# Nine of 24 units: y turned through DRAM and VectorE in place of TensorE

## The chip, the cores and the metric

The kernel runs on one core of one Trainium2 chip. The metric is device time in microseconds, from the start of the program to its end; the median of several runs is compared. A profiled execution also leaves a trace, whose span goes from its first to its last instruction.

## The reference

Two blocks are computed one after the other. The first is an mLSTM cell over `q`, `k`, `v` of shape (4, 8, 768, 40), with input, forget and output gates. At each time step and for each head:

```
m_new  = max(f + m, i)
C      = exp(f + m - m_new) * C + exp(i - m_new) * outer(v, k)
n      = exp(f + m - m_new) * n + exp(i - m_new) * k
y      = sigmoid(o) * (C q) / max(|n . q|, 1)
```

The y of all heads, 8 x 40 = 320 values for each of 4 x 768 = 3072 tokens, is the input x of a multiplicative feed-forward block with 1024 inner features, whose result (3072 x 320) is the output:

```
a, b = x @ w1, x @ w2
out  = ((a * b) @ w3) @ w_out
```

All is float32.

## The kernel before

**Tiling.** The cell works on units of 128 tokens of one batch: 6 chunks of 128 tokens by 4 batches make 24 units, numbered 0 to 23, batch fastest. Within a unit the recurrence is computed in two halves of 64 tokens: score matmuls within a half, a carried state between halves. Four units, one for each batch, make a group, so there are 6 groups. `w3 @ w_out` is folded once into `w3o`, so that the feed-forward block has an up stage (`up`, `up_rest`: a and b for pairs of feature tiles over 256 tokens, and their product `ab`) and a down stage (`ffn_out`: `po`, accumulated over the eight feature tiles for 128 tokens at a time).

**Steps.** One loop over s from 0 to 29 staggers all of this. In step s the cell begins unit s (scores and state, `quarter_work`) and ends unit s-1 (`outputs`, which writes y, 128 tokens by 320 values, at L382). Step s then holds, for earlier units, the turn of y, and feed-forward work set by the lists `n_up` and `n_down`: two up pieces a step from s = 7 to 28, and two down pieces a step from s = 17 to 26. Group 3 (units 12 to 15) is read by the up stage in steps 17 to 20, group 4 in steps 21 to 24, group 5 in steps 25 to 28; the first two steps of each read the group's first two units, the last two its other two. Step 29 holds the last four down pieces.

**The turn of y.** The up matmuls need x with features on partitions. In step s, `twice` (GpSimd, L386) writes the last 64 columns of unit s-2's y a second time, so that the 320 features make three tiles of 128. One step later `x_trans` turns the three tiles with TensorE (L93) into one PSUM tile `px`, and ScalarE copies it to `xT` (L396), which holds 512 tokens of a group and has two buffers.

**Other turns.** The q and k of the first 17 units are turned by TensorE (`turn`, `pt`). From unit 17 on (`N_DVE`), `load_turned` loads them with eight DMAs a unit into `turned_in` (single, in the tile `gates`), in an arrangement in which VectorE's transposes of 32x32 blocks finish the job (L287).

**PSUM.** The cell tile takes four banks. `mps` gives the other four, pool `ps_m`, to `px`, `pt`, `pa`, `pb`, `po` in turn. After step 24 the cell tile is closed and its four banks become a second pool, `ps_x`; from then `mps` takes the two pools by turns:

```
pool = banks.pop(0)
banks.append(pool)
return pool.tile(shape, FP, name=name, tag="m")
```

**What sets the order.** TensorE's order is the order of the program (`in_order`). The other engines' instructions, the DMA issues on SyncE's queue among them, are ordered by a scheduler from program order and its own estimate of when each is ready; each queue then runs in that order and waits at its head. In the first seven steps the program order is kept (`keep_order`). From step 1 to 24 the part after `quarter_work` that turns k and q on VectorE is held behind the last VectorE instruction of `outputs` (`issue_after(gated.ins)`). In the program, a step begins with the loads: weights for three units on (`load_u`, tile `pw`), k, q, v and the output gate two units on (`load`, `load_o`); `load_o` takes the buffer that y of unit s-2 frees. The y tile has two buffers, `o_sb`, which takes the result out, has two as well.

Of the kernel before, what the change touches and what calls it, by code (L numbers as in the profile page):

```python
# [8 lines left out]
FP = mybir.dt.float32  # L9
# [7 lines left out]
def kernel(  # L17
# [26 lines left out]
    nc = tc.nc  # L44
# [3 lines left out]
    P = 128  # L48
    NT = S // L
    NT2 = S // P  # L50
    NU = NT2 * B
# [3 lines left out]
    DM = H * D  # L55
# [3 lines left out]
    KF = DM // P  # L59
    REM = DM - KF * P  # L60
    GT = B
    TG = GT * P
# [5 lines left out]
    sb = ctx.enter_context(tc.tile_pool(name="sb", bufs=2))  # L68
    dram = ctx.enter_context(tc.tile_pool(name="dram", bufs=1, space=bass.MemoryType.DRAM))
# [39 lines left out]
    wT = const.tile([P, NT2, BH], FP, name="wT")  # L109
    decay = const.tile([P, B * NP, NT], FP, name="decay")  # L110
    U_d = dram.tile([NT, BH, L], FP, name="U_d")
    KC = KF + 1

    o_t, u_t = {}, {}

# [4 lines left out]
    def load(n):  # L120
        for dst, src in ((kbuf[n % NB][:, :, 0:D], k), (qbuf[n % NBQ][:, :, 0:D], q), (vbuf[n % NB][:, :, 0:D], v)):
            if src is not q or n < N_DVE:
                nc.sync.dma_start(out=dst, in_=rows(src, n))

    def load_turned(n):
        c, b = divmod(n, B)
        for dst, src in zip(turned_in, (k, q)):
            for hip in range(2):
                of = src[b].rearrange("(p two) s d -> two p s d", two=2)[hip, :, c * P:(c + 1) * P, :]
                for j in range(2):  # L130
                    p0, c0 = hip * DP + j * 32, (1 - j) * 32
                    nc.sync.dma_start(out=dst[p0:p0 + 32, c0:c0 + NP * RAW].rearrange("r (p e) -> r p e", p=NP),
                                      in_=of.rearrange("p (r f) d -> r p (f d)", f=4))

    def load_o(n):
        o_t[n] = io.tile([P, H, D], FP, name="o_in", tag="o_in", bufs=4)
        nc.sync.dma_start(out=o_t[n], in_=rows(o_gate, n))

    def load_u(n):
        c, b = divmod(n, B)  # L140
        src = U_d[2 * c:2 * c + 2, b * H:(b + 1) * H, :].rearrange("x h t -> x (h t)")
        for x in range(2):
            nc.sync.dma_start(out=weights_tile(n)[halves[x]].rearrange("p h t -> p (h t)"),
                              in_=src[x:x + 1].to_broadcast([L, H * L]))
# [77 lines left out]
    def scale_next():  # L222
        scaled.append(pend.pop(0))
        scale(scaled[-1][1])
# [17 lines left out]
    def fold():  # L242
        while ready_w3:
            w3_mm(ready_w3.pop(0))
        ready_w3.extend(turned_w3)
        turned_w3.clear()
# [9 lines left out]
    qT_t, kT_t, vw_t, before_t, y_t, x_t = {}, {}, {}, {}, {}, {}  # L256

    def out_gate(n):
        nc.scalar.activation(out=o_t[n], in_=o_t[n], func=AF.Tanh, scale=0.5)
# [11 lines left out]
    def weights(n):  # L271
        c, b = divmod(n, B)
        src = weights_tile(n) if c else spread(n)
        pw = weights_tile(n)
        for h in range(H):
            nc.scalar.activation(out=pw[:, h, :], in_=src[:, h, :], func=AF.Exp, bias=aT[:, c, b * H + h:b * H + h + 1])  # L276
        for r in halves:
            nc.gpsimd.affine_select(out=pw[r], in_=pw[r], compare_op=OP.is_ge, fill=0.0, base=0,  # L278
                                    pattern=[[0, H], [1, L]], channel_multiplier=-1)

    def turn(n):


        if n >= N_DVE:
            for src, dst, name in zip(turned_in, (kT_t, qT_t), ("kT", "qT")):
                dst[n] = sb.tile([128, NP, P], FP, name=name, tag=name)
                nc.vector.transpose(out=dst[n].rearrange("i p (r f) -> i p f r", f=4),  # L287
                                    in_=src[:, 32:TB].rearrange("i (p f d) -> i p f d", p=NP, f=4)[:, :, :, 0:32])
            return
        for src, dst, name in ((kbuf[n % NB], kT_t, "kT"), (qbuf[n % NBQ], qT_t, "qT")):  # L290
            pt = mps([128, NP, P], "pt")
            for p in range(NP):
                transpose(pt[:, p, :], src[:, 2 * p:2 * p + 2, :].rearrange("p a b -> p (a b)"))
            dst[n] = sb.tile([128, NP, P], FP, name=name, tag=name)
            nc.scalar.copy(out=dst[n], in_=pt)

    def weighted(n):
        c, b = divmod(n, B)
        vw_t[n] = sb.tile([P, H, D1], FP, name="vw", tag="vw")
        nc.gpsimd.tensor_tensor(out=vw_t[n], in0=vbuf[n % NB], op=OP.mult,  # L300
                                in1=wT[:, c, b * H:(b + 1) * H].unsqueeze(2).to_broadcast([P, H, D1]))

    def decayed(new, old, n, x):
        c, b = divmod(n, B)
        nc.gpsimd.tensor_tensor(out=new, in0=old, op=OP.mult, in1=decay[:, b * NP:(b + 1) * NP, 2 * c + x:2 * c + x + 1]  # L305
                                .to_broadcast([P, NP, D1]))
# [55 lines left out]
    def outputs(n, pi, ph):  # L362
# [6 lines left out]
        for x, r in enumerate(halves):  # L369
# [12 lines left out]
        return nc.vector.tensor_tensor(out=y_t[n][:, 0:DM].rearrange("p (h d) -> p h d", d=D), in0=h[:, :, 0:D], in1=e,  # L382
                                op=OP.mult)

    def twice(n):
        nc.gpsimd.tensor_copy(out=y_t[n][:, DM:DM + REM], in_=y_t[n][:, KF * P:DM])  # L386

    def x_trans(n):
        gr, j = divmod(n, GT)
        if j == 0:  # L390
            x_t[gr] = ffn.tile([128, KF + 1, TG], FP, name="xT", tag="xT")
        y = y_t.pop(n)
        px = mps([128, KF + 1, P], "px")
        for cc in range(KF + 1):
            transpose(px[:, cc, :], y[:, cc * P:(cc + 1) * P])
        nc.scalar.copy(out=x_t[gr][:, :, j * P:(j + 1) * P], in_=px)  # L396
# [119 lines left out]
    ffn = ctx.enter_context(tc.tile_pool(name="ffn", bufs=2))  # L516
# [27 lines left out]
    def ffn_out(gr, j):  # L544
        po = mps([P, DM], "po")
        for f in range(FO):
            mm(po, ab_t[gr][j // 2][:, f, j % 2 * P:(j % 2 + 1) * P], w3o[:, f, :], start=(f == 0), stop=(f == FO - 1))
        o_sb = ffn.tile([P, DM], FP, name="o_sb", tag="o_sb", bufs=2)
        nc.scalar.copy(out=o_sb, in_=po)  # L549
        t0 = j * S + gr * P  # L550
        nc.scalar.dma_start(out=out[t0:t0 + P, :], in_=o_sb)
# [13 lines left out]
    turned, converted, fetched = 0, 2, 2 * KF + 1  # L565

    for s in range(len(n_up)):
        if B <= s + 3 < NU:
            load_u(s + 3)
        if s + 2 < NU:  # L570
            load(s + 2)
            load_o(s + 2)
        if 0 < s < B - 1:
            weights(s + 1)
            out_gate(s)
        if s < NU:
            weighted(s)
            if s >= B:
                decayed(state[s % B][1], state[s % B][0], s, 0)
            if 0 < s < N_DVE:  # L580
                turn(s)
        if 0 <= s - 2 < NU:
            twice(s - 2)
        if N_DVE <= s + 1 < NU:
            load_turned(s + 1)
        while turned < min(s - 2, NU):
            x_trans(turned)
            turned += 1
        fold()
        for _ in range(n_down[s]):  # L590
            ffn_out(*downs.pop(0))
        now = [ups.pop(0) for _ in range(n_up[s])]
        open_ups = [up(*x) for x in now]
        if len(now) == 1 and turned == s - 2 < NU:
            x_trans(turned)
            turned += 1

        def rest():
            for x in open_ups:
                up_rest(*x)  # L600

        gated = None
        if s <= NU:
            gated = quarter_work(s, rest)
        else:
            rest()
        with tc.issue_after(gated.ins) if gated else nullcontext():
            if N_DVE <= s + 1 < NU:
                turn(s + 1)
        if s == 0:  # L610
            gate_cols(g, gT, nc.scalar.copy)
            out_gate(0)
            scale_next()
            weights(1)
        if s == NU:
            cell_psum.close()
            banks.append(ctx.enter_context(tc.tile_pool(name="ps_x", bufs=4, space=bass.MemoryType.PSUM)))
        if B - 1 <= s < NU:
            if s + 1 < NU:
                weights(s + 1)  # L620
            out_gate(s)
        for _ in range(n_cvt[s] if s < len(n_cvt) else 0):
            convert()
            converted += 1
        while todo and fetched < converted + (2 if s < 2 else 3):
            fetch(*todo.pop(0))
            fetched += 1
        if s + 1 == pinned:
            for ins in keep_order(front):
                behind.enter_context(tc.issue_after(ins))  # L630
# [30 lines left out]
```

## Time and profile before

| | us |
|---|---|
| median of 5 runs | 490.55 |
| lowest, highest run | 490.43, 492.9 |
| the profiled execution's own time | 492.14 |
| its span, first to last instruction | 490.4 |
| TensorE matmuls busy | 457.2 |
| VectorE busy | 261.0 |
| ScalarE busy | 146.3 |
| GpSimd busy | 88.2 |

The shares are averages over stages. Until about 230 us the weights are also loaded and converted on VectorE, and q and k are turned on TensorE; after that the steps are alike. In rows of groups of instructions, PE is a matmul and PEld the load of its stationary operand, DVE is VectorE, ACT ScalarE, POOL GpSimd and SPq SyncE's DMA queue. In a row of waits, the engine and line that waited come first, then what it waited for, the sum in us, the number of times and the longest. In a row of the timeline, the start comes first (us from the span's start), then the time, and in brackets the idle time before it and what ended it.

The DMA engines are busy to 42.2% of the span with 112,528 packets on the queue that carries SyncE's loads. The transposes of y take 72 matmuls (13.6 us by the sum of their durations), the copies to `xT` 11.6 us of ScalarE, the doubling of the last columns 7.3 us of GpSimd.

### The profile page before, as it was taken

How to read it: one execution, taken by the hardware profiler on the slowest of the kernel's cores; microseconds unless marked ns; L12 is line 12 of the kernel's file. 1: busy time of each engine (PE TensorE's matmuls, PEld its weight loads, DVE VectorE, ACT ScalarE, POOL GpSimd, SP SyncE). 2: the span in 40 equal slices, each digit the busy share in tenths (PEclk: the TensorE clock that was granted, in tenths of full speed). 3: DMA queues.
4: the chain of work that ended last, by engine and by line, in shares of the span. 5: the costliest groups of instructions: out<-in, count | busy, mean ns of one | idle time of the engine just before them, and what ended most of it. 6: DMA issues, size and time to landing. Idle time of an engine off the chain costs nothing.

```text
span 490.4 us, 13366 instructions
## 1 busy us (share of the span) xinstructions
PE 457.2 (93%) x5658; PEld 375.1 (76%) x5658; DVE 261.0 (53%) x526; ACT 146.3 (30%) x399; POOL 88.2 (18%) x165
## 2 busy tenths in 40 slices
PE   3859797979899999999999999999999998999997
PEld 2748796979687887888877787777877777777864
DVE  7786689899859788877660615325144042011110
ACT  3642643633433442524531313212101011011011
POOL 5431222702303211322320201111000000000000
PEclk9996988989899999999999999999999999999999
DMA  9899927689955947630452325233120000000001
GB/s 188 158 187 206 170 69 139 125 159 181 194 103 133 169 112 142 137 76 20 94 103 72 83 63 142 51 94 72 39 80 3 27 15 15 28 13 15 1 13 40
DMA packets 116188, 45.76 MB, mean 93 GB/s; under 512 B 96737, under 2 KB 107169, under 8 KB 116129
## 3 DMA queue, kind: packets, MB, share of 16 engines
q1 hardware_dynamic: 112528, 40.88, 42.2%
q10 hardware_dynamic: 3600, 4.03, 2.4%
q8 instruction: 44, 0.72, 0.6%
q14 instruction: 16, 0.12, 0.1%
HBM read 40.86 MB, written 4.03 MB: 92 GB/s over the span
## 4 chain that ended last, share of the span: by engine, by line
PE 78%; issue 8%; DVE 6%; DMA 3%; SPq 2%; POOL 2%; ACT 1%; POOLq 0%; ACTq 0%
PE pa L90 22%; PE po L90 21%; PE pb L90 15%; PE cell L90 8%; PE wp L90 7%; PE pt L93 2%; SPq L168 2%; PE px L93 1%; DMA raw<-in_moe_w_out_dram 1%; DVE h L370 1%; DMA kbuf<-in_k_dram 1%; PE ub L90 1%; POOL pw L278 1%; DMA raw<-in_moe_w_dram 1%; DVE o_in L380 1%
## 5 line engine op out<-in xcount | busy, mean ns | idle before, releaser
L542 DVE TENSOR_TENSOR ab<-pb,a_sb 128x512 f32<-128x512 f32 x48 | 33.0, 690 | 165.2 <-ACT a_sb L541 165.1
L90 PE MATMUL po<-w3o,ab 128*128 128x320 f32 x384 | 105.4, 433 | 1.3 <-DVE h L370 1.3
L90 PEld LDWEIGHTS po<-w3o,ab 128*128 128x128 f32 x384 | 72.2, 190 | 30.7 <-issue 1.5
L90 PE MATMUL pa<-xT,w 128*128 128x256 f32 (+1 forms) x448 | 95.1, 361 | 0.6 <-ACT xT L396 0.6
L90 PE MATMUL pb<-xT,w 128*128 128x256 f32 (+1 forms) x448 | 92.2, 352 | 0.0
L90 PEld LDWEIGHTS pa<-xT,w 128*128 128x128 f32 x448 | 79.2, 202 | 11.7 <-ACT xT L396 1.0
L90 PEld LDWEIGHTS pb<-xT,w 128*128 128x128 f32 x448 | 76.8, 194 | 8.3
L541 ACT ACTIVATE a_sb<-pa 128x512 f32<-128x512 f32 x48 | 28.6, 596 | 148.6 <-PE pb L90 148.6
L90 PE MATMUL pa<-xT,wr 64*64 64x256 f32 (+1 forms) x448 | 48.2, 357 | 0.0
L90 PE MATMUL pb<-xT,wr 64*64 64x256 f32 (+1 forms) x448 | 48.2, 357 | 0.0
L305 POOL TENSOR_TENSOR state<-state,decay 128x164 f32<-128x164 f32 x40 | 19.3, 486 | 153.3 <-PE cell L90 96.0
L278 POOL TENSOR_SCALAR_AFFINE_SELECT pw<-pw 64x512 f32<-64x512 f32 x48 | 37.0, 771 | 46.2 <-ACT pw L276 43.8
L276 ACT ACTIVATE pw<-pw,aT 128x64 f32<-128x64 f32 x160 | 40.5, 339 | 8.8 <-DMA pw<-U_d 8.8
L90 PEld LDWEIGHTS pa<-xT,wr 64*64 64x64 f32 x448 | 29.2, 136 | 15.1 <-issue 7.2
L90 PE MATMUL wp<-wo,w3T 128*128 128x320 f32 x128 | 37.5, 449 | 2.0 <-DVE w3T L237 2.0
L90 PEld LDWEIGHTS wp<-wo,w3T 128*128 128x128 f32 x128 | 24.7, 198 | 11.8 <-issue 3.4
L549 ACT COPY o_sb<-po 128x320 f32<-128x320 f32 x24 | 10.2, 424 | 67.3 <-PE po L90 63.3
L90 PEld LDWEIGHTS cell<-vbuf,pw 64*64 64x64 f32 x768 | 26.4, 136 | 4.0 <-issue 1.8
L90 PEld LDWEIGHTS pb<-xT,wr 64*64 64x64 f32 x448 | 29.2, 136 | 0.0
L90 PE MATMUL cell<-vbuf,pw 64*64 64x41 f32 x768 | 26.3, 226 | 1.4 <-issue 1.4
L386 POOL COPY y<-y 128x64 f32<-128x64 f32 x24 | 7.3, 303 | 109.9 <-DVE y L382 106.1
L346 DVE TENSOR_TENSOR pw<-cell,pw 128x512 f32<-128x512 f32 x24 | 16.4, 685 | 17.1 <-PE cell L90 14.0
(89 smaller groups left out, 510.0 us busy)
## 6 DMA issues: line engine op xcount, KB each, us to landing
raw<-in_moe_w_dram SPq DMA_DIRECT2D x64, 128.0 KB, 3.2
pw<-U_d SPq DMA_DIRECT2D x40, 128.0 KB, 3.5
kbuf<-in_k_dram SPq DMA_DIRECT2D x24, 160.0 KB, 4.4
vbuf<-in_v_dram SPq DMA_DIRECT2D x24, 160.0 KB, 4.7
o_in<-in_o_gate_dram SPq DMA_DIRECT2D x24, 160.0 KB, 3.4
out_dram<-o_sb ACTq DMA_DIRECT2D x24, 160.0 KB, 1.8
raw<-in_moe_w_dram SPq DMA_DIRECT2D x7, 512.0 KB, 5.7
qbuf<-in_q_dram SPq DMA_DIRECT2D x17, 160.0 KB, 4.8
```

What stands on the lines that cost most here:

```text
L90: in_order(nc.tensor.matmul(out, lhsT=lhsT, rhs=rhs, start=start, stop=stop))
L93: in_order(nc.tensor.transpose(out, in_, ident[0:n, 0:n]))
L168: nc.sync.dma_start(out=dst, in_=src)
L276: nc.scalar.activation(out=pw[:, h, :], in_=src[:, h, :], func=AF.Exp, bias=aT[:, c, b * H + h:b * H + h + 1])
L278: nc.gpsimd.affine_select(out=pw[r], in_=pw[r], compare_op=OP.is_ge, fill=0.0, base=0, pattern=[[0, H], [1, L]], channel_multiplier=-1)
L305: nc.gpsimd.tensor_tensor(out=new, in0=old, op=OP.mult, in1=decay[:, b * NP:(b + 1) * NP, 2 * c + x:2 * c + x + 1] .to_broadcast([P, NP, D1]))
L346: first_read = nc.vector.tensor_tensor(out=pv, in0=ss, in1=pv, op=OP.mult)
L370: nc.vector.tensor_tensor(out=h[r], in0=ph[x], in1=h[r], op=OP.add)
L386: nc.gpsimd.tensor_copy(out=y_t[n][:, DM:DM + REM], in_=y_t[n][:, KF * P:DM])
L541: nc.scalar.mul(out=a_sb, in_=pa, mul=UP ** -2)
L542: nc.vector.tensor_tensor(out=ab_t[gr][j][:, fs[0]:fs[-1] + 1, t0:t0 + a_sb.shape[-1]], in0=pb, in1=a_sb, op=OP.mult)
L549: nc.scalar.copy(out=o_sb, in_=po)
```

## The change

For units 15 to 23 (`NY` = 15) the turn of y leaves TensorE. In step s, for unit s-2: `send` stores y in DRAM with four DMAs (1,536 runs of 32 values, the last 64 columns twice, once for each half of the partition quarters), `get_back` loads it with four DMAs into a new tile `yb` (one buffer), with the four 32-column pieces of each feature tile on the four quarters of the partitions, and `x_turn` turns the 32x32 blocks with one VectorE instruction straight into `xT`. `x_turn` stands where the k and q turns stand, ahead of them, and behind the last VectorE instruction of `outputs` in the same step. `send` stands after the step's loads on SyncE, `get_back` after `load_turned`. The transposes by TensorE, the ScalarE copy and `twice` are left out for these units; for units 0 to 14 nothing changes. Group 3's `xT` is so written by ScalarE for units 12 to 14 and by VectorE for unit 15.

```diff
+    NY = 15
     KC = KF + 1
+    y_d = [dram.tile([P, 4, KC, 32], FP, name=f"y_d{n}") if n >= NY else None for n in range(NU)]
...
+    def send(n):
+        y = y_t.pop(n)
+        for cc in range(KF):
+            nc.sync.dma_start(out=y_d[n][:, :, cc, :], in_=y[:, cc * P:(cc + 1) * P].rearrange("t (i c) -> t i c", c=32))
+        for i in range(0, 4, 2):
+            nc.sync.dma_start(out=y_d[n][:, i:i + 2, KF, :], in_=y[:, KF * P:DM].rearrange("t (i c) -> t i c", c=32))
+
+    back_t = {}
+
+    def get_back(n):
+        back_t[n] = sb.tile([P, 4, KC, 32], FP, name="yb", tag="yb", bufs=1)
+        for i in range(4):
+            nc.sync.dma_start(out=back_t[n][32 * i:32 * (i + 1)].rearrange("r m k c -> r m (k c)"),
+                              in_=y_d[n][:, i].rearrange("(m r) k c -> r m (k c)", r=32))
+
+    def x_turn(n):
+        gr, j = divmod(n, GT)
+        if j == 0:
+            x_t[gr] = ffn.tile([128, KC, TG], FP, name="xT", tag="xT")
+        nc.vector.transpose(out=x_t[gr][:, :, j * P:(j + 1) * P].rearrange("c k (m r) -> c k m r", r=32),
+                            in_=back_t.pop(n).rearrange("r m k c -> r k m c"))
...
-        if 0 <= s - 2 < NU:
+        if NY <= s - 2 < NU:
+            send(s - 2)
+        elif 0 <= s - 2 < NY:
             twice(s - 2)
         if N_DVE <= s + 1 < NU:
             load_turned(s + 1)
-        while turned < min(s - 2, NU):
+        if NY <= s - 2 < NU:
+            get_back(s - 2)
+        while turned < min(s - 2, NY):
             x_trans(turned)
             turned += 1
...
-        if len(now) == 1 and turned == s - 2 < NU:
+        if len(now) == 1 and turned == s - 2 < NY:
             x_trans(turned)
             turned += 1
...
         with tc.issue_after(gated.ins) if gated else nullcontext():
+            if NY <= s - 2 < NU:
+                x_turn(s - 2)
             if N_DVE <= s + 1 < NU:
                 turn(s + 1)
```

## The prediction

> **What bounds the kernel now.** I read the page first: busy shares and the forty slices, then the granted clock by stretch. TensorE's matmul row is busy for 457.2 of 490.4 us. A busy matmul row can hide slack, because matmuls overlap, so I asked for the busy time in stretches cut at the start of each unit's cell matmuls, from the 17th step on. Columns: length of the stretch, then PE, PEld, DVE, ACT, POOL busy (instructions), granted clock, DMA share, GB/s.
>
> ```profile
> PE 457.2 (93%) x5658; PEld 375.1 (76%) x5658; DVE 261.0 (53%) x526; ACT 146.3 (30%) x399; POOL 88.2 (18%) x165
> ...
> 271.50:291.71 20.21, 20.21 (x231) 15.98 (x227) 7.54 (x16) 4.90 (x14) 3.22 (x6) 1.00 0.37 88
> 352.32:372.51 20.19, 20.19 (x215) 15.98 (x211) 7.20 (x14) 2.52 (x5) 0.98 (x2) 1.00 0.18 50
> 412.91:434.00 21.09, 19.80 (x169) 15.13 (x164) 4.72 (x11) 2.60 (x6) 0.24 (x1) 1.00 0.05 16
> ```
>
> Six steps in a row last 20.2 us with no matmul gap, at full granted clock, whatever the DMA share is (0.37 or 0.05). VectorE is idle for 12 to 13 us of each. So here the end is set by the sum of TensorE's issue times alone: what leaves TensorE comes off the end, and what goes to VectorE or the DMA is free until it holds TensorE up. The one stretch with a gap is 412.91 to 434.00. The waits from 250 us to the end name it; hardly any other wait of TensorE is there:
>
> ```profile
> PEld pa L90 <- issue: 4.0, 12, 0.3
> PEld po L90 <- issue: 1.5, 1, 1.5
> PE po L90 <- DVE h L370: 1.3, 1, 1.3
> ```
>
> **What a set of three transposes costs.** The page's mean of 300 ns for one is a latency and overlaps its neighbours. I take starts from the timeline of TensorE: start, duration, idle before. The same joint, last up matmul to first `po` matmul, occurs with the transposes (433 us) and without them (469 us):
>
> ```profile
> 433.50 0.38 PE L90 MATMUL pb<-xT,wr 64*64 64x256 f32 x1
> 433.80 0.55 PE L93 MATMUL px<-ident,y 128*128 128x128 f32 x3
> 434.18 1.24 PE L90 MATMUL po<-w3o,ab 128*128 128x320 f32 x4
> ...
> 469.37 0.38 PE L90 MATMUL pb<-xT,wr 64*64 64x256 f32 x1
> 469.67 1.34 PE L90 MATMUL po<-w3o,ab 128*128 128x320 f32 x4
> ```
>
> With: 434.18 - 433.50 = 0.68. Without: 469.67 - 469.37 = 0.30. A set costs 0.38 us. The joint after cell matmuls agrees: `px` starts at 273.94 and `po` at 274.32, again 0.38.
>
> **What the Trainium skill says.** "VectorE: DVE Perf Modes", section "The three transpose paths": VectorE turns only separate 32x32 blocks and writes to SBUF. That is why y must go through DRAM: the blocks have to change places. The trace has two such instructions, L237 (mean 709 ns) and L287 (1119 and 1095), both 128x512. "DMA: Bandwidth & Descriptors", section "Two DMAs through the same engine are not ordered": a read of what another DMA wrote must wait on that DMA's completion. So the loads back wait on SyncE for the stores; before has such a pair only at its start, far from the stretch at issue. Same page, "Specifications": below 512 B a transfer pays a read-modify-write. The change stores 128 B runs and reads 384 B runs; the existing 160 B row loads show what such runs cost here, 3.4 to 4.8 us to land.
>
> **The change, part by part.**
>
> Removed from TensorE: units 15 to 23 are nine units, so nine sets of three transposes. 9 x 0.38 = 3.42 us, all in the gap-free part.
>
> Removed from the PSUM rotation: nine `px` tiles. `mps` takes pools in turn, and after step 24 it alternates between `ps_m` and the new `ps_x`, which stands on the banks of the closed cell tile. In step 25 the first tile asked for is `px` (unit 22), from `ps_m`; the first `po` falls on `ps_x` and waits for the last VectorE reads of the cell banks:
>
> ```profile
> 414.39 0.55 PE L93 MATMUL px<-ident,y 128*128 128x128 f32 x3
> 416.23 4.01 PE L90 MATMUL po<-w3o,ab 128*128 128x320 f32 x14 [1.29 <-DVE h L370]
> ```
>
> Without `px`, this first `po` comes from `ps_m` and can start about 414.39. The second `po` takes `ps_x` 4.31 us later, near 418.7, when the reads (the second `h` add starts at 415.58 and takes about half a us) are over. This joint so gains 416.23 - 414.39 = 1.84 us: its 0.38 and 1.46 for the wait. Earlier, four banks turn with six tiles a step in place of seven. The first `po` then takes the bank of the previous step's first `pa`, which ScalarE has read by about 271.5 in the step where `po` starts at 274.3; taking the set out brings that to about 273.9, still later. The last pairs `pa` and `pb` wait for the same `o_sb` copies as now, with about 4 us to spare (copy over at 283.57, `pb` at 288.12). Cost: none.
>
> Removed from ScalarE and GpSimd: nine `xT` copies of 485 ns and nine y copies of 303 ns. Both engines wait there; worth nothing.
>
> Added to SyncE: four stores and four loads a unit, 72 in all. Each is 196,608 B per unit and direction: 1,536 runs of 128 B out, 512 of 384 B in. The page gives 42.2% of 16 engines over 490.4 us for 112,528 packets, which is 29 ns a packet; 2,048 packets are an estimated 3.8 us over 16 engines, or 0.19 of a step on top of at most 0.38. SyncE's queue in one step:
>
> ```profile
> 279.09 0.37 SPq L137 DMA_DIRECT2D o_in<-in_o_gate_dram  x1
> 280.13 1.98 SPq L132 DMA_DIRECT2D gates<-in_k_dram  x4
> 282.20 1.80 SPq L132 DMA_DIRECT2D gates<-in_q_dram  x4
> 292.87 1.09 SPq L143 DMA_DIRECT2D pw<-U_d  x2
> ```
>
> Four issues take about 1.8 us. The y of the unit is done at 279.07. Stores: issued by 281.3. Landing: the only store of gates to DRAM takes a median 3.1 us, the row loads up to 4.8; I take 3.1. In that time the eight turned loads go out, from 281.3 to 285.1. Then the four loads back go out to 286.9 and land after 2.6 us (the 80 KB `gates` loads): about 289.5, 10.5 us after y. What is queued behind their wait is the next step's loads, which start at 292.87 anyway. With 4.8 us for both landings it is about 292: still nothing late.
>
> Added to VectorE: nine block transposes of 128x384. No row has this shape; scaled from 512 elements it is an estimated 0.53 us (L237's rate) to 0.84 (L287's). I take 0.7, 6.3 us in all. They stand after the next unit's y and ahead of its k and q transposes, here:
>
> ```profile
> 298.78 0.49 DVE L382 TENSOR_TENSOR y<-h,o_in 128x320 f32<-128x320 f32 x1
> 299.19 1.11 DVE L287 STREAM_TRANSPOSE kT<-gates 128x512 f32<-128x512 f32 x1
> 300.14 1.09 DVE L287 STREAM_TRANSPOSE qT<-gates 128x512 f32<-128x512 f32 x1
> 311.92 0.69 DVE L542 TENSOR_TENSOR ab<-pb,a_sb 128x512 f32<-128x512 f32 x1 [10.68 <-ACT a_sb L541]
> ```
>
> The data is there near 289.5, VectorE comes to it at 299.2, so it waits for nothing. The 10.68 us idle after `qT` hides it; without that cover it would cost 0.7 a unit. The k and q transposes, pushed by 0.7, feed score matmuls about 14 us later. The turned `xT` of a unit is read two steps after it is written, about 20 us; the last unit has no cell step behind it, and its reader is at 451.69.
>
> Sum: 8 x 0.38 + 1.84 = 4.88 us. Profiled execution: span 490.4 becomes 485.5 and its own 492.14 becomes 487.26. It stands 1.59 above the median of the runs, 490.55; since the steps priced here ran at full clock, I take the same 4.88 off the median: **485.7 us**.
>
> **The rivals.** *A: only the transposes.* The cell-bank wait moves to another `po`, or the scheduler gives the first `po` the late banks anyway. For it: slots are chosen by a scheduler whose view I can't see. Against: the pool order is fixed by `mps`. 490.55 - 3.42 = 487.1. *B: the saving is eaten by in-order waits on ScalarE.* ScalarE already waits up to 3.1 us for landing `pw` and `o_in` ahead of its `o_sb` copies; new stores share those queues. Beyond about 4 us more, the last `pb` waits for its bank. Losing some 0.5 us in each of nine steps gives about 490. Against: `o_in` is issued ahead of the stores. *C, slower: the trip through DRAM ends after VectorE has reached the transpose.* VectorE then holds kT of the next step, and TensorE stops at the score matmuls. It starts to cost where the trip takes about 32 us from y instead of 10.5 (next y about 20 us on, plus 14 us to the score matmuls, less 2 us of k and q transposes); at 33.5 us eight steps lose 1.5 us each, 12 us less 4.9 saved: 497.7. For it: a serial store, wait, load with small runs, never seen in this stretch. Against: the DMA engines are at most 0.38 busy.
>
> **How the numbers follow.** Forecast 0.76, A 0.12, B 0.06, C 0.06. The forecast's own range is 484.9 to 486.3: the joint after cell matmuls is known to some 0.1 us a set, and a median moves by a few tenths (the runs before lie from 490.43 to 492.9, most of them close to the lower end). The range 484.7 to 487.4 takes in A and leaves out B and C. About 0.3%, 1.5 us, is what a measurement can tell from no change. Faster: forecast and A, 0.88. Within 0.3%: most of B, 0.05. Slower: C and the rest, 0.07.
>
> **What would show it.** Right: `px` counts 45 matmuls, not 72; steps from 274 us on last 19.8 us; no wait of `po` on `h`; transposes into `xT` with no DMA wait ahead of them. Wrong: VectorE idle ahead of `xT` on the loads back, TensorE idle on kT or `xT`, a longer `o_in` wait with `pb` late, or a reordered SyncE queue in which the loads back delay loads for the next unit.

## The result and the profile after

The changed kernel takes 487.15 us in the median of its runs, 490.26 us the kernel before in the runs beside it. The ratio, 0.9931 with a 95% interval from 0.9913 to 0.995, is taken over fast runs alone, those no more than 1.5% above their kernel's fastest; both profiled executions lie above that, but the stretches compared below ran at full granted clock. By this ratio the change is worth 2.5 to 4.3 us; 4.88 us were forecast. The span of the profiled execution went from 490.4 to 486.5 us.

The page of the changed kernel, and from its groups the rows that the edit touches (busy us, mean ns, then idle before and what ended it):

```profile
span 486.5 us, 13400 instructions
...
PE 455.6 (94%) x5631; PEld 373.2 (77%) x5631; DVE 265.1 (54%) x535; ACT 141.8 (29%) x390; POOL 85.9 (18%) x156
```

```profile
L93 PE MATMUL px<-ident,y 128*128 128x128 f32 x45 | 8.8, 302 | 5.3 <-DVE y L384 5.3
L408 DVE STREAM_TRANSPOSE xT<-yb 128x384 f32<-128x384 f32 x9 | 5.1, 571 | 6.1 <-DMA yb<-y_d 6.1
```

45 transposes are left of 72, and VectorE has nine new ones of 571 ns. Its only wait on the loads back is at the last unit, where it has nothing else to do. The stretches of the changed kernel, cut at the first cell matmul of a step as before:

```profile
271.67:291.59 19.92, 19.92 (x228) 15.70 (x224) 8.00 (x16) 4.42 (x13) 2.94 (x5) 1.00 0.49 109
351.35:371.27 19.92, 19.92 (x212) 15.69 (x208) 7.65 (x15) 2.04 (x4) 0.74 (x1) 1.00 0.30 70
411.10:430.40 19.30, 19.30 (x165) 14.84 (x160) 5.80 (x13) 2.14 (x5) 0.00 (x0) 1.00 0.17 39
```

A step is 19.92 us, still without a gap, where 20.20 us was before and 19.82 us was forecast. The DMA share rose from 0.37 to 0.49 and TensorE felt nothing. The stretch with the gap lost it. TensorE's timeline there:

```profile
411.10 1.02 PE L90 MATMUL cell<-vbuf,pw 64*64 64x41 f32 x30
...
412.58 8.88 PE L90 MATMUL po<-w3o,ab 128*128 128x320 f32 x32
421.30 1.89 PE L90 MATMUL pa<-xT,w 128*128 128x256 f32 x8
```

The first `po` starts with the cell matmuls' end and carries no wait on `h`. The whole gain, by starts of the same instruction in both timelines:

| stretch | before | after | gained |
|---|---|---|---|
| seven steps, cell matmuls of step 17 to those of step 24 | 271.51 to 412.91 | 271.67 to 411.10 | 1.97 |
| to the first `pa` of step 25 | to 424.91 | to 421.30 | 1.80 |
| to the first `pa` of step 26 | to 442.80 | to 438.90 | 0.29 |
| to the end | to 490.4 | to 486.5 | 0.0 |

The sum is 4.06 us, less 0.16 us by which this execution reached 271 us later: the 3.9 us between the spans. The seven steps at 0.28 us each, with 0.29 in step 26, are what falls short of the forecast.

### The profile page after: what moved, and what is told of

Same layout as the page of the kernel before. It is cut to its first block, busy times and chain, and to the rows that moved or that the text cites. A ratio compares the mean times of both kernels' runs of the same rounds, so it can differ in the third digit from the quotient of the medians.

```text
span 486.5 us, 13400 instructions
## 1 busy us (share of the span) xinstructions
PE 455.6 (94%) x5631; PEld 373.2 (77%) x5631; DVE 265.1 (54%) x535; ACT 141.8 (29%) x390; POOL 85.9 (18%) x156
## 4 chain that ended last, share of the span: by engine, by line
PE 75%; DVE 8%; issue 8%; SPq 3%; DMA 2%; POOL 2%; ACT 1%; POOLq 0%; DVEq 0%
PE po L90 22%; PE pa L90 21%; PE pb L90 14%; PE cell L90 8%; PE wp L90 7%; SPq L170 2%; PE pt L93 2%; DVE h L372 1%; DMA raw<-in_moe_w_dram 1%; DMA kbuf<-in_k_dram 1%; PE ub L90 1%; DVE o_in L382 1%; POOL pw L280 1%; DVE ma L189 1%; DVE h L368 1%
## 5 line engine op out<-in xcount | busy, mean ns | idle before, releaser
L90 PE MATMUL pa<-xT,w 128*128 128x256 f32 (+1 forms) x448 | 94.1, 358 | 0.6 <-ACT xT L422 0.6
L90 PEld LDWEIGHTS pa<-xT,w 128*128 128x128 f32 x448 | 78.1, 198 | 11.7 <-ACT xT L422 1.0
L278 ACT ACTIVATE pw<-pw,aT 128x64 f32<-128x64 f32 x160 | 40.6, 339 | 17.4 <-DMA pw<-U_d 17.4
L90 PEld LDWEIGHTS wp<-wo,w3T 128*128 128x128 f32 x128 | 24.6, 197 | 11.8 <-issue 3.4
L90 PEld LDWEIGHTS cell<-vbuf,pw 64*64 64x64 f32 x768 | 27.4, 141 | 4.2 <-issue 2.0
L90 PE MATMUL cell<-vbuf,pw 64*64 64x41 f32 x768 | 27.3, 230 | 1.4 <-issue 1.4
L372 DVE TENSOR_TENSOR h<-cell,h 64x328 f32<-64x328 f32 x48 | 23.8, 496 | 1.0
```

The costliest lines, as they stand in the source:

```text
L90: in_order(nc.tensor.matmul(out, lhsT=lhsT, rhs=rhs, start=start, stop=stop))
L372: nc.vector.tensor_tensor(out=h[r], in0=ph[x], in1=h[r], op=OP.add)
```

## The experiments

**A step gained 0.28 us, not 0.38.** Here is the joint behind the cell matmuls of step 17 in the timelines of TensorE, first before, then after:

```profile
273.94 0.55 PE L93 MATMUL px<-ident,y 128*128 128x128 f32 x3
274.32 8.78 PE L90 MATMUL po<-w3o,ab 128*128 128x320 f32 x32
282.94 1.89 PE L90 MATMUL pa<-xT,w 128*128 128x256 f32 x8
```

```profile
274.10 8.88 PE L90 MATMUL po<-w3o,ab 128*128 128x320 f32 x32
282.82 1.89 PE L90 MATMUL pa<-xT,w 128*128 128x256 f32 x8
```

Now `po` starts just where `px` used to start, 2.43 us after the first cell matmul (271.51 before, 271.67 after), so its start did move by 0.38. But its 32 matmuls now last 8.72 us to the first `pa` (282.82 - 274.10), not 8.62 (282.94 - 274.32). The theory: the first matmul on the whole array after 64x64 tiles costs 0.10 us more, and the transposes used to pay it. The rival: the transposes were simply cheaper than thought. I put back one transpose, or three, for units 15 to 21, into a PSUM tile that nothing reads. VectorE still makes `xT`, so the extra transposes are work added to the changed kernel.

```diff
-        y = y_t.pop(n)
+        y = y_t[n]
...
+        if NY <= s - 3 < 22:
+            y = y_t.pop(s - 3)
+            px = mps([128, KF + 1, P], "px")
+            for cc in range(1):                     # 3 in the second kernel
+                transpose(px[:, cc, :], y[:, (cc % KF) * P:(cc % KF + 1) * P])
         fold()
```

> The changed kernel, with one TensorE transpose of y put back for units 15 to 21, into a PSUM tile that nothing reads (VectorE still makes xT). This asks why a step fell by 0.285 us, not by 0.38. Theory: the first matmul on the whole 128x128 array after the cell's 64x64 tiles pays about 0.10 us, which the first po pays when no transpose stands ahead of it; a lone transpose takes that over. Then a step is 19.92 - 0.10 + 0.16 = 19.98 us, and the 32 po matmuls take 8.62 us again, start of po to start of pa, in place of 8.72. Rival: each transpose is simply worth 0.095 us in place of 0.127: a step of 20.015 us, po stays at 8.72.

> The same with all three transposes of units 15 to 21 put back on TensorE, still unread, so that ScalarE's copy to xT stays out and the trip through DRAM and VectorE stays in. If the saving of a step is TensorE's issue time alone, a step is 20.20 us again with po at 8.62, whatever ScalarE, VectorE and the DMA do. If part of the 0.285 us came from ScalarE's missing copy, or if the added DMA took some of it, a step lies visibly off 20.20 us (by 0.05 or more).

TensorE's timeline with one transpose, and with three:

```profile
287.40 1.02 PE L90 MATMUL cell<-vbuf,pw 64*64 64x41 f32 x30
...
289.82 0.33 PE L93 MATMUL px<-ident,y 128*128 128x128 f32 x1
289.99 8.78 PE L90 MATMUL po<-w3o,ab 128*128 128x320 f32 x32
298.61 1.67 PE L90 MATMUL pa<-xT,w 128*128 128x256 f32 x7
```

```profile
286.73 1.02 PE L90 MATMUL cell<-vbuf,pw 64*64 64x41 f32 x30
...
289.22 0.55 PE L93 MATMUL px<-ident,y 128*128 128x128 f32 x3
289.60 8.78 PE L90 MATMUL po<-w3o,ab 128*128 128x320 f32 x32
298.22 1.89 PE L90 MATMUL pa<-xT,w 128*128 128x256 f32 x8
```

One lone transpose brings `po` back to 8.62 us (298.61 - 289.99). The step is (407.29 - 287.40) / 6 = 19.98 us, as the theory had it, where the rival had 20.015. So the first transpose adds 0.06 us to the step and the other two together 0.23: with three, (407.99 - 286.73) / 6 = 20.21 us. That is the step of the kernel before, with ScalarE's copies still out and the trip through DRAM still in. Both are free; TensorE's issue time is the whole account of these steps.

The extra 0.10 us can be seen in the loads of the stationary operands (PEld). First the changed kernel, then the one with a single transpose:

```profile
274.10 0.19 PEld L90 LDWEIGHTS po<-w3o,ab 128*128 128x128 f32 x1
274.10 0.54 PE L90 MATMUL po<-w3o,ab 128*128 128x320 f32 x1
```

```profile
289.82 0.14 PEld L93 LDWEIGHTS px<-ident,y 128*128 128x128 f32 x1
289.82 0.33 PE L93 MATMUL px<-ident,y 128*128 128x128 f32 x1
289.83 0.36 PEld L90 LDWEIGHTS po<-w3o,ab 128*128 128x128 f32 x2
...
289.99 0.43 PE L90 MATMUL po<-w3o,ab 128*128 128x320 f32 x1
```

In the changed kernel the load of the first `po` behind the tiles starts together with its matmul, which then takes 0.54 us in place of 0.43, and the next one starts 0.37 us later in place of 0.27; inside a row of `po` each load starts 0.27 us ahead of its matmul. With one transpose in between, the load goes ahead of the matmul by 0.16 us and the matmul takes 0.43. It is the same at all twelve places from 268 us on where the changed kernel goes from 64x64 tiles to the whole array: none of these loads starts more than 2 ns ahead. So what a transpose takes over is a load that nothing hides; its own costs less (0.33 us in place of the median 0.27). The tiles need not be the only occasion: before, in step 25, the first `po` comes behind transposes on the whole array and a wait, its load starts at 416.19 and its matmul at 416.23, and the 32 matmuls last 8.68 us (424.91 - 416.23). Why a load behind tiles starts no earlier is not shown.

**The wait on the cell's banks.** Two edits move the pool that the first `po` of step 25 gets, one in each direction. In the changed kernel the order of the pools is turned round:

```diff
         if s == NU:
             cell_psum.close()
-            banks.append(ctx.enter_context(tc.tile_pool(name="ps_x", bufs=4, space=bass.MemoryType.PSUM)))
+            banks.insert(0, ctx.enter_context(tc.tile_pool(name="ps_x", bufs=4, space=bass.MemoryType.PSUM)))
```

> The changed kernel, with the two PSUM pools in the other order from step 25 on, so that the first po of that step comes from the banks of the closed cell tile. If the wait that the change lost came from the pool order, this po waits again for the second h add (which ends near 414.3 in the trace of the changed kernel, against a po start of 412.58): a wait of po on h of about 1.3 us as the trace counts it, the stretch from the cell matmuls of step 24 to the first pa of step 25 grows from 10.20 us to about 12.0, and the whole is about 1.8 us slower than the changed kernel, nothing else moves. Rival: the wait had another cause that the missing transposes removed; then the stretch stays at 10.20 us and the time at that of the changed kernel.

In the kernel before, the first tile after the close doesn't move the rotation, so `px` and the first `po` both come from `ps_m`:

```diff
+    hold = []
     def mps(shape, name):
+        if hold:
+            hold.pop()
+            return banks[0].tile(shape, FP, name=name, tag="m")
...
             banks.append(ctx.enter_context(tc.tile_pool(name="ps_x", bufs=4, space=bass.MemoryType.PSUM)))
+            hold.append(1)
```

> The kernel before, with one edit: in step 25 the px tile and the first po both come from ps_m, and the pools alternate only from then on. All 24 units are still turned by TensorE. If the bank is what the po waits for, the wait of 1.3 us on h is gone and the stretch from the cell matmuls of step 24 to the first pa of step 25 falls from 12.00 us to about 10.5 (10.20 of the changed kernel and a set of transposes, 0.28): about 1.5 us faster than before, that is 0.3% or a ratio near 0.997. Steps 17 to 24 stay at 20.2 us. Rival: no wait goes and the ratio is 1.000.

The timeline of TensorE in step 25, of the first kernel and then of the second (whose lines are shifted by five):

```profile
410.67 1.02 PE L90 MATMUL cell<-vbuf,pw 64*64 64x41 f32 x30
...
413.98 8.85 PE L90 MATMUL po<-w3o,ab 128*128 128x320 f32 x32 [1.77 <-DVE h L372]
422.67 1.89 PE L90 MATMUL pa<-xT,w 128*128 128x256 f32 x8
```

```profile
408.32 1.02 PE L95 MATMUL cell<-vbuf,pw 64*64 64x41 f32 x30
...
409.80 0.55 PE L98 MATMUL px<-ident,y 128*128 128x128 f32 x3
410.18 8.78 PE L95 MATMUL po<-w3o,ab 128*128 128x320 f32 x32
418.80 1.89 PE L95 MATMUL pa<-xT,w 128*128 128x256 f32 x8
```

With the pools turned round, the wait is back and the stretch from cell matmuls to `pa` is 12.00 us, to the hundredth that of the kernel before, though no transpose stands in it. So in this one place the transposes were free: they ran inside a wait that ended when VectorE had read `h`. In the second kernel, with all 72 transposes still there, the wait is gone and the stretch is 10.48 us: 1.52 us for a change of one bank. The whole times say the same less sharply: ratios to before of 0.9988 (0.9964 to 1.0012) and 0.9979 (0.9946 to 1.0013), neither resolved from 1 by itself.

**How long the trip may take.** Serial copies from DRAM to DRAM between store and load lengthen it, two in one kernel, five in the other:

```diff
+    HOPS = 2                                        # 5 in the other
+    y_h = [[dram.tile([P, 4, KC, 32], FP, name=f"y_h{n}_{i}") for i in range(HOPS + 1)] if n >= NY else None for n in range(NU)]
+    y_d = [x and x[0] for x in y_h]
...
     def get_back(n):
+        for i in range(HOPS):
+            nc.sync.dma_start(out=y_h[n][i + 1], in_=y_h[n][i])
         back_t[n] = sb.tile([P, 4, KC, 32], FP, name="yb", tag="yb", bufs=1)
         for i in range(4):
             nc.sync.dma_start(out=back_t[n][32 * i:32 * (i + 1)].rearrange("r m k c -> r m (k c)"),
-                              in_=y_d[n][:, i].rearrange("(m r) k c -> r m (k c)", r=32))
+                              in_=y_h[n][HOPS][:, i].rearrange("(m r) k c -> r m (k c)", r=32))
```

> The changed kernel, with two copies from DRAM to DRAM of each y between the stores and the loads back, each issued by SyncE after the one before it has landed: a longer trip, nothing else. In the trace of the changed kernel y of unit 16 is done at 279.2, the loads back are issued until 288.0 and should land near 290.5; VectorE comes to the transpose at 299.1. At an estimated 3 us for a copy the trip ends near 296.5, still ahead of VectorE: the time of the changed kernel, steps of 19.92 us. Rival: the trip is already near the limit (or the added traffic matters), and steps grow.

> The same with five copies, so that the trip is some 26 us. The prediction's slow case says that a trip costs nothing until about 32 us after y, since only VectorE's order counts: then the time is that of the changed kernel still, with a wait of VectorE on the loads back of some 6 us a unit. Rival: SyncE is one queue that stands still during the trip, so the limit is the step of 19.92 us less its other issues; at 26 us the next units' loads of k and q come later with each unit, TensorE waits on the score matmuls, and steps become some 25 us: 10 to 35 us slower in all.

The ratios to before are 0.9897 (0.9862 to 0.9932) and 0.9913 (0.9883 to 0.9942), both like the changed kernel. Steps are 19.92 us in both: (408.21 - 268.78) / 7 and (410.63 - 271.20) / 7. VectorE's timeline with five copies:

```profile
298.19 0.49 DVE L386 TENSOR_TENSOR y<-h,o_in 128x320 f32<-128x320 f32 x1
298.60 1.13 DVE L291 STREAM_TRANSPOSE kT<-gates 128x512 f32<-128x512 f32 x1
...
305.13 0.58 DVE L412 STREAM_TRANSPOSE xT<-yb 128x384 f32<-128x384 f32 x1 [4.43 <-DMA yb<-y_h]
...
330.52 0.58 DVE L412 STREAM_TRANSPOSE xT<-yb 128x384 f32<-128x384 f32 x1 [9.95 <-DMA yb<-y_h]
```

Unit 16's y was done at 278.76, so its trip took 26.4 us; unit 17's took 31.8 us (298.68 to 330.52). VectorE stands up to 9.95 us at the load, inside its idle time, and TensorE doesn't notice. Both theories on record missed something here. My rival's SyncE queue does not stand still for a whole trip: the scheduler laid the copies of one unit between the issues of the next. And it put the k and q transposes ahead of the one into `xT`, so the late load could not hold them, and the limit of 32 us, drawn for the other order, was not put to the test.

**VectorE's cover.** Each transpose into `xT` eight times:

```diff
-        nc.vector.transpose(out=x_t[gr][:, :, j * P:(j + 1) * P].rearrange("c k (m r) -> c k m r", r=32),
-                            in_=back_t.pop(n).rearrange("r m k c -> r k m c"))
+        back = back_t.pop(n)
+        for _ in range(8):
+            nc.vector.transpose(out=x_t[gr][:, :, j * P:(j + 1) * P].rearrange("c k (m r) -> c k m r", r=32),
+                                in_=back.rearrange("r m k c -> r k m c"))
```

> The changed kernel, with each of the nine VectorE transposes into xT made eight times over (same input, same output): seven more of 0.57 us, some 4 us more of VectorE a step, ahead of the k and q transposes. If the 10 us that VectorE stands idle before ab hide it, steps stay at 19.92 us and the idle time before ab falls from 9.94 to about 6 us. Rival: TensorE feels VectorE's later k and q transposes or the later xT, and steps grow by up to 4 us.

The idle time before `ab` fell from 9.94 us as expected:

```profile
289.12 0.69 DVE L570 TENSOR_TENSOR ab<-pb,a_sb 128x512 f32<-128x512 f32 x1 [6.03 <-ACT a_sb L569]
```

Steps stay at 19.92 us. VectorE's share of the change costs nothing here, with room for at least seven times as much. The rival, later k and q transposes, was hardly tested: the scheduler laid only one of the eight ahead of k (277.18), a second between k and q, and six behind q (278.57).

**More units.** If a set is worth 0.28 us wherever TensorE is full, earlier units should pay too:

```diff
-    NY = 15
+    NY = 12                                         # 9, 11 in the others
```

> The changed kernel with the change from unit 12 on (12 units in place of 9). Three more sets leave TensorE: at 0.28 us each, 0.85 us faster than the changed kernel if VectorE and the DMA still have room in steps 14 to 16, in which weights are still loaded and converted. Rival: in that stage VectorE and SyncE's queue are what is full, and the gain is lost there: no faster, or slower.

> The same from unit 9 on (15 units). Six more sets than the changed kernel: 1.7 us faster than it if nothing else gives. Rival as with unit 12, more strongly: from step 11 on VectorE is busy for 9 to 13 of 16.8 us a step with conversions, and SyncE waits at its head for buffers of raw weights, so that the added stores, waits and loads delay weights: slower than the changed kernel by a us or more.

> The change from unit 11 on (13 units), between the case from unit 12, which gained, and that from unit 9, which lost since VectorE made a transpose one step late behind the weight conversions and TensorE waited for xT. If unit 11 still fits, it is 0.28 us faster than from unit 12 on, with no wait of TensorE on xT. If VectorE's order already puts the transpose of unit 11 a step late, TensorE waits for it in step 15 by one to four us, and the case is slower than from unit 12 on by that much.

| units turned by VectorE | ratio to before | from y of unit 11 to y of unit 23, us |
|---|---|---|
| none (before) | 1 | 228.56 |
| 15 to 23 (the change) | 0.9931 (0.9913 to 0.995) | 226.52 |
| 12 to 23 | 0.9874 (0.9834 to 0.9913) | 225.58 |
| 11 to 23 | 0.9987 (0.9962 to 1.0013) | 228.41 |
| 9 to 23 | 1.0123 (1.0087 to 1.0159) | 234.49 |

The last column takes the starts of the y instructions in each profile. From unit 12 on the stretch is 0.94 us shorter than with the change, near the 0.85 expected: by this column the best of these kernels. Two whole-time intervals that meet at 0.9913 don't rank it by themselves. From unit 9 on, TensorE's waits between 186 and 230 us name the slow rival, and VectorE's timeline shows its place:

```profile
PEld pa L90 <- issue: 7.6, 4, 4.2
PE pa L90 <- DVE xT L408: 5.9, 2, 3.8
```

```profile
171.12 0.49 DVE L384 TENSOR_TENSOR y<-h,o_in 128x320 f32<-128x320 f32 x1
...
186.85 0.49 DVE L384 TENSOR_TENSOR y<-h,o_in 128x320 f32<-128x320 f32 x1
187.26 0.57 DVE L408 STREAM_TRANSPOSE xT<-yb 128x384 f32<-128x384 f32 x1
```

The first transpose into `xT` belongs to unit 9, whose y started at 154.27 and whose loads back were issued by 166.02. The program places it after y of unit 10 (171.12); on VectorE it stands a step later, at 187.26, and the next up stage waits for it: `pa` starts at 187.98 after a wait on `xT`. `yb` has one buffer, so unit 10's loads back go out only then (187.86) and the delay is handed on. Whether a second `yb` buffer would cure this was not tried, and why the scheduler laid the transpose a step late stays open.

From unit 11 on TensorE shows no wait on `xT` from 180 to 260 us. It stops once, in the fold of w3 (the two rows of waits are one stop, of the weight load and of the matmul):

```profile
PEld wp L90 <- ACT pw L278: 3.2, 1, 3.2
PE wp L90 <- DVE w3T L239: 3.0, 1, 3.0
```

```profile
248.59 4.54 PE L90 MATMUL wp<-wo,w3T 128*128 128x320 f32 x16 [3.04 <-DVE w3T L239]
```

The changed kernel and the one from unit 12 on have no such wait in this stretch. The one stop accounts for the lost gain: the kernel from unit 12 on gained 0.94 us, a further set about 0.3, and with 3.04 us lost the stretch should be 1.8 us longer than the changed kernel's; it is 1.89. From y of unit 16 to y of unit 23 it takes 136.71 us, the changed kernel 136.74, so nothing is lost later. A late transpose came before this stop too. The one of unit 11 belongs behind y of unit 12 (200.93) and stands at 217.04, just ahead of y of unit 13. It holds `yb`, and SyncE's queue stands 11.8 us at unit 12's loads back, with loads of raw weights behind them:

```profile
204.84 0.40 SPq L170 DMA_DIRECT2D raw<-in_moe_w_dram  x1
217.64 2.50 SPq L401 DMA_DIRECT2D yb<-y_d  x4
220.19 1.37 SPq L170 DMA_DIRECT2D raw<-in_moe_w_dram  x3
```

Counted from y of unit 11, these last three loads go out after 34.4 us, and after 21.2 us in the kernel from unit 12 on (208.59); the last VectorE transpose of w3 comes after 62.0 us, there after 53.4. That the queue's stop causes the late w3 fits both figures but was not tried by itself: ScalarE also scales the last part of w3 late in its order (242.91, behind an `a_sb`), and there early (236.68, ahead of it). In the kernel from unit 12 on the first two transposes come late too, about 12 us after the next y, and no wait of TensorE follows.

## Why the prediction was right, and where a size was off

**What bounds the kernel** held: steps without a gap before and after, and three transposes put back bring 20.21 us again, whatever the other engines and the DMA do.

**The whole time: right only in the wider range.** The median of 487.15 us lies outside the forecast's own 484.9 to 486.3. It lies in 484.7 to 487.4 because that takes in rival A, whose mechanism did not come. The traces show 4.06 us gained in the part that was priced; the medians differ by 3.1 us, and the first 190 us vary from one execution to the next by more than the difference between the two.

**The set of three, 0.38 us: mis-sized.** It is worth 0.285 us. The step that failed is the comparison of joints: I took the time to the *start* of the first `po` and assumed that what follows is the same. It is not, by 0.10 us. The lines that I showed held it: four `po` matmuls lasted 1.24 us behind the transposes and 1.34 us behind the up matmuls. Measured to the next instruction that is alike on both sides, the joint would have given 0.28. Eight sets were put at 3.04 us and measured 2.26 (1.97 and 0.29): 0.78 of the 0.82 us that the sum was too high. The other 0.04 is in step 25. The 13.6 us given with the profile before would have misled too: it is the time in which at least one of the 72 transposes was under way (72 of 300 ns are 21.6), 0.57 us a set, twice what a set is worth.

**The bank's wait, 1.84 us with its set: right.** It measured 1.80. It is 44% of the gain of 4.06 us, and comes from an edit that nobody would call its subject: one tile fewer in a rotation. Undone, it gives back all 1.8 us; done alone, it gains 1.52, where I had put 1.46 for the wait and 0.38 for the set.

**DMA, SyncE, VectorE at nothing: right**, by wide margins. A trip of 31.8 us and eight transposes a unit left the step at 19.92. The transposes took 0.57 us (I took 0.7, between 0.53 and 0.84). The DMA share of a step grew by 0.12, where I had estimated 0.19. Stores landed in a median 2.6 us (64 KB) and 1.9 us (32 KB), the loads back in 2.1 us. SyncE did wait for the stores ahead of the loads back, 3.7 us in five waits from 260 to 430 us. Unit 16's loads back were issued by 287.97, so that its trip from y (279.23) ended near 290.1 by the median landing, 10.8 us in place of 10.5. The trip of the last unit, with no turned loads in between, ran from y at 415.97 to 422.58: 6.6 us. That y must go through DRAM, because the blocks have to change places, was not put to a test: no run took another way.

**The rivals.** A's number, 487.1, is the median measured, but that is chance: A kept the bank's wait, and it went. B did not come: ScalarE waited 17.4 us for `pw` in place of 8.8, and no `pb` was late. C did not come in this kernel; late transposes that make TensorE wait came from unit 9 on, where VectorE converts weights, and through VectorE's order, not through a long trip. Its limit of 32 us was drawn for an order of VectorE that the scheduler changed where five copies made the loads late.

## What to carry to other kernels

Price the removal of an instruction on a full engine between two instructions that are the same on both sides, beyond its neighbours: what it leaves behind may cost more without it. Look for what a removed tile does to a rotation of buffers; here one place in it was worth six sets of transposes. A free engine makes a move free only where it is free: the same edit that gained from unit 12 on lost its gain from unit 11 on, and more than that from unit 9 on, where VectorE was at work on weights and its transposes came late. And a buffer that is single ties a DMA queue to the engine that reads it: one late transpose kept weight loads waiting for 11.8 us.

## What was not expected of the hardware

The load of the first full-array operand behind 64x64 tiles starts only with its own matmul, at all twelve such places of the changed kernel from 268 us on. A `po` matmul there takes 0.54 us in place of 0.43 and holds up the next by 0.10 us, with 32 `po` at 8.72 in place of 8.62 us; one 128x128 transpose in between takes that over at a net 0.06 us. And the first 190 us vary from one execution to the next far more than the change is worth: y of unit 11, up to which these kernels do the same work, starts at 188.80 and 188.96 us in the profiles before and after, and at 184.20 with the banks alone changed. The differences between later starts repeat to a few hundredths of a us, so the stages, not the whole time, carried the small verdicts here.
